# A gated mix of a state-space layer and an MLP on one core: the first two pairs of w1 tiles by halves of 256 tokens

## The chip, the cores and the metric

The kernel runs on one core of a Trainium2 chip. The metric is the device time of one execution in microseconds (us); lower is better. The engines are called by the profile's names: PE (TensorE's matmuls), PEld (its weight loads), DVE (VectorE), ACT (ScalarE), POOL (GpSimd) and SP (SyncE, which here only issues DMAs). SPq, ACTq and POOLq are the queues on which these engines issue DMAs.

## The reference

The input x has 2048 tokens of 448 values in bf16. Three things are computed from it and mixed:

```python
def _A_ref(x, Lambda_re, Lambda_im, B_re, B_im, C_re, C_im, log_dt, Dskip):
    ...
    dt = jnp.exp(log_dt)
    Lam_bar = jnp.exp(dt * Lam)                      # 448 complex poles
    B_bar = ((Lam_bar - 1.0) / Lam)[:, None] * Bmat
    Bu = jnp.einsum("bld,pd->blp", x + 0j, B_bar)    # 448 -> 448 complex
    for t in range(L):
        h = Lam_bar[None, :] * h + Bu[:, t, :]
        hs.append(h)
    y = 2.0 * jnp.einsum("blp,dp->bld", hseq, Cmat).real + x * Dskip[None, None, :]
    return y

def _B_ref(x, w1, w2):
    h = jnp.einsum("bsd,df->bsf", x, w1)             # 448 -> 1792
    h = _silu(h)
    return jnp.einsum("bsf,fd->bsd", h, w2)          # 1792 -> 448

g = _sigmoid((x * gate_w).sum(-1, keepdims=True))
return g * a + (1 - g) * b                           # a = _A_ref, b = _B_ref
```

## The kernel before

**Tiles and stages.** The tokens are cut into four chunks of 512 (`CH`). x lies in `xnat` with tokens on partitions (16 blocks of 128) and is transposed on PE into `xT`, with features on partitions. The 448 features are cut at columns 0, 128, 256 and 320 (`XCOL`) into four pieces `i`; the pieces of `xT` are used by halves of 64 partitions, and two matmuls of 64 rows, one on the upper and one on the lower rows of the array, run beside each other, for two different output tiles. Such a pair of tiles takes 14 matmuls of 64 x 128 weights and 512 tokens, 7 for each tile: first four pairs of matmuls (`part[0]`), then three (`part[1]`), in which the two tiles have changed rows. An output tile is 128 columns of w1 (kind `F`, 14 of them a chunk) or 128 rows of B (kind `B`, 7 of them).

`x_products` (L654) makes these products for a list of tiles, two at a time. `steps(k, h, a, z)` is one group of matmuls of pair `k`; `half(k, h)` is its first or second half, and after the second `evict` takes the two PSUM banks to SBUF: `F` tiles through SiLU on ACT into `aT`, `B` tiles into `UG`. The halves of neighbouring pairs alternate: first half of pair k+1, then second half of pair k. The later stages are `lanes` (the recurrence, as a rotation by COS and SIN, a scan on DVE and a rotation back), `ffn2` (L775, the product with w2), `readout_weights` and `readout` (L796, the product with C), and `gates`.

**The order of the work.** A planner (`Plan`) holds a list of operations with costs, priorities and what they read and write. PE takes its operations in exactly the order in which the code adds them; on SP, ACT, DVE and POOL the planner picks, by its own costs, the operation that can start first and, among these, the one of lowest priority number. `Waits` turns the result into one instruction list per engine with semaphore waits. An engine runs its list in order: an instruction that waits holds all behind it. PE does not wait for itself, except in an operation marked `own`: there it waits until its earlier writes to the bank are done (the second half of a pair adds to a bank from the other rows).

**The start, which the change touches.** Loads (all from `load`, L387 to L390) are issued in the order of their priority numbers: x's tokens 0 to 255 (`xn00`) on SP and 256 to 511 (`xn01`) on ACT; the first 256 columns of w1 (`w1cuts[0:2]`, tiles 0 and 1 of kind `F`) as pieces 0 and 1 on SP, piece 2 and piece 3 on ACT; three rows of parameters (`prm`) on SP; then on SP w1's columns 256 to 511, 512 to 767 and 768 to 1023, two loads each, then B (`Bnat`, which lies in the buffer of `H[3]`; the real part, then the imaginary part `A_B_im`), the rest of w1, the gate and skip vectors, and the rest of x, w2 and C. POOL begins with an iota and a compare that make the identity matrix `ident` (L443, L444), then an iota and cast for the phase (L445, L446), and signs.

PE begins with `warm` (L461): `NWARM` = 6 matmuls of ones with 512 columns and one with 256, whose result is not used. Then come four groups of eight transposes, `x0_transposes(q0, part, who)` (L468 to L478), two for each 256 tokens (`part` 0 and 1), two for the pieces 0, 1 and 2, 3. Each group goes to two banks, and a copy on DVE ("d") or ACT ("a") takes each into `xT` (L486, L488). Then `fill` (L497 to L499), two matmuls of ones with 256 columns, and then the first half of the first pair, cut in two for the loads of w1.

`parameters` (L536) turns the three rows `prm` into columns: a copy of 64 of their columns on DVE (L545), four small matmuls on PE (L543), a copy (L547), and then a long chain on POOL, DVE and ACT that ends in `COS`, `SIN` and the scale factors. It is added behind the first half of the first pair. `b_transposes` (L600 to L611) transposes B in two batches among the products of the third to fifth pair; the second needs the last load of `A_B_im`.

Of the kernel before, what the change touches and what calls it, by code (L numbers as in the profile page):

```python
# [8 lines left out]
AF = mybir.ActivationFunctionType  # L9
# [13 lines left out]
NOT = 5  # L23
NWARM = 6
NFILL = 2
# [251 lines left out]
def bass_gated_mix__ssm_conv_s5__dense_activation_silu__prompt_kernel(nc, A_x, A_Lambda_re, A_Lambda_im, A_B_re, A_B_im, A_C_re, A_C_im,  # L277
               A_log_dt, A_Dskip, B_x, B_w1, B_w2, gate_w, out):
    with ExitStack() as ctx:
# [78 lines left out]
        def bk(t, k=0):  # L358
            return ps[:, t.bank + k, :]
# [22 lines left out]
        def PE(fn, r, w, cost, tag=""):  # L382
            return P.add("pe", fn, r, w, cost, 0, tag=tag)
# [16 lines left out]

        for h, q in enumerate(("sp", "act")):
            load(q, xnat[:, 2 * h:2 * h + 2, :], x2[256 * h:256 * h + 256, :].rearrange("(b p) d -> p b d", p=128), f"xn0{h}", 256 * 896)
        load_w1("sp", 0, 0, 2)
        load_w1("act", 0, 2, 3)
        load_w1("act", 0, 3, 4)
        for k, v in enumerate((A_log_dt, A_Lambda_re, A_Lambda_im)):
            load("sp", prm[k:k + 1, 0:448], v.rearrange("(o n) -> o n", o=1), f"prm{k}", 896)
        for k in range(1, len(w1cuts) - 2):
# [59 lines left out]
        def x0_transposes(q0, part, who):  # L468

            tk = Ps(2)  # L470

            def mm(pe):
                for q in (q0, q0 + 1):
                    for k in range(2):
                        o = ((q - q0) * 2 + k) * 64
                        for h in range(2):
                            p = slice(64 * h, 64 * h + 64)
                            r = pe.transpose(bk(tk, h).bitcast(BF16)[:, o:o + 64], xnat[p, 2 * part + k, XCOL[q]:XCOL[q] + 128], ident[p, p])  # L478
# [12 lines left out]
        x0_transposes(0, 1, "da")  # L491
        x0_transposes(2, 0, "da")
        x0_transposes(2, 1, "dd")

# [7 lines left out]
        xn_of = {tc: {q: [f"xT{tc}_{h}" for h in range(2)] for q in range(4)} for tc in range(1, NCH)}  # L502
        xn_of[0] = {q: [f"xT0_{q}{part}{h}" for part in range(2) for h in range(2)] for q in range(4)}

# [31 lines left out]
        def parameters():  # L536
# [4 lines left out]
            def prm_t(pe):  # L541
                for b in range(4):
                    r = pe.matmul(bk(tkp)[:, 4 * b:4 * b + 3], prm[0:3, 128 * b:128 * b + 128], ident[0:3, 0:3], start=True, stop=True)  # L543
# [110 lines left out]
        def x_products(tiles, fill={}, wait=()):  # L654
# [9 lines left out]

            def steps(k, h, a, z):
                def body(pe):
                    for n, cut in list(enumerate(part[h]))[a:z]:
                        for b, ((i, p0), tile) in enumerate(zip(cut, pairs[k])):
                            tc = tile[1]
                            r = pe.matmul(bk(toks[k], b), weights(tile, p0, p0 + 64, i), xT[p0:p0 + 64, i, tc * CH:(tc + 1) * CH],  # L670
                                          start=(h == 0 and n == 0), stop=(h == 1 and n == 2))
                    return r
                reads = [n for cut in part[h][a:z] for (i, _), tile in zip(cut, pairs[k])
                         for n in xn_of[tile[1]][i] + (w1n(tile[2], i) if tile[0] == "F" else btn[tile[2]])]
                return PE(body, list(dict.fromkeys(reads)), [toks[k]], (z - a) * PE_MM[512], f"{pairs[k][0][0]}{pairs[k][0][1]}")

            def half(k, h):
                if h == 0 and pairs[k][0] == ("F", 0, 0):
                    steps(k, 0, 0, 2)
                    steps(k, 0, 2, 4)  # L680
                else:
                    steps(k, h, 0, len(part[h])).own = h == 1
                if h:
                    evict(pairs[k], toks[k])

            half(0, 0)
            for f in fill.get(-1, ()):
                f()
            for k in range(len(pairs)):
                order = [lambda: half(k, 1)] + [lambda: half(k + 1, 0)] * (k + 1 < len(pairs))  # L690
# [229 lines left out]
```

## Time and profile before

| what | before |
|---|---|
| time, three runs | 142.47, 143.05, 144.9 us; median 143.05 us |
| the profiled execution: its time, and its span | 142.07 us, 140.2 us |
| PE busy | 136.7 us, 97% of the span |
| DVE, ACT, POOL busy | 123.2, 89.0, 38.7 us |
| products with w1 and B (L670), busy | 48.6 + 25.8 us |
| products with w2 (L775), busy | 43.4 us |
| products with C (L796), busy | 16.4 us |
| DMA moved | 14.71 MB, 105 GB/s on average |

The span runs from the first to the last instruction that the profile counts; the execution's own time is 1.87 us longer. Busy time of PE counts each matmul from its start to its modelled end, and two matmuls on different rows overlap, so the mean time of one matmul is longer than the distance from one to the next. The timeline gives start, length, engine, line, operation and operands of merged neighbours; in brackets stands how long the engine had been idle, and what released it. A stage table gives for stretches of time the busy share of each engine, the share of the DMA engines and the GB/s that they moved. Times in the text are from the span's start.

### The profile page before, as it was taken

The page shows a single profiled execution, that of the slowest core. Times are in us where ns is not written, and L with a number is a line of the kernel's source. Part 1 is how long each engine was busy: PE and PEld are TensorE (multiplying, and loading weights), DVE is VectorE, ACT ScalarE, POOL GpSimd, SP SyncE. Part 2 cuts the span into 40 slices and gives each one's busy share as a digit, 9 for nine tenths or more (in the row PEclk, how much of TensorE's full clock was granted, in tenths as well). Part 3 has the DMA queues.
Part 4 walks back from the last instruction along what each step waited for, and adds up shares of the span by engine and source line. Part 5 has one row for each costly group of instructions (what it writes and reads, how often), then busy time and mean ns, then how long its engine had stood idle before and what let it go on. Part 6 is the DMA issues. An engine that isn't in the chain of part 4 may idle for free.

```text
span 140.2 us, 3002 instructions
## 1 busy us (share of the span) xinstructions
PE 136.7 (97%) x1199; PEld 67.5 (48%) x1199; DVE 123.2 (88%) x179; ACT 89.0 (63%) x155; POOL 38.7 (28%) x72
## 2 busy tenths in 40 slices
PE   7999999999999999999999999999999999999992
PEld 2445554445544544455554544444455555555561
DVE  0369999999999999999999999999699999599153
ACT  3239758999998998713971886899920068412300
POOL 7160004201545600229560002833000204222220
PEclk9999999999999999999999999999999999999999
DMA  4988999820447730108975000947001402245342
GB/s 142 262 254 251 320 380 271 201 55 0 69 78 123 126 45 0 37 0 127 158 142 139 0 5 0 134 92 115 2 2 57 106 0 37 33 98 120 46 94 70
DMA packets 18500, 14.71 MB, mean 105 GB/s; under 512 B 2867, under 2 KB 18358, under 8 KB 18486
## 3 DMA queue, kind: packets, MB, share of 16 engines
q0 software_dynamic: 6064, 5.51, 24.7%
q1 hardware_dynamic: 11862, 8.65, 20.4%
q10 hardware_dynamic: 560, 0.36, 0.8%
q8 instruction: 9, 0.15, 0.5%
q14 instruction: 5, 0.04, 0.1%
HBM read 7.17 MB, written 1.84 MB: 64 GB/s over the span
## 4 chain that ended last, share of the span: by engine, by line
PE 97%; DVE 0%; issue 0%
PE ps L670 46%; PE ps L775 31%; PE ps L796 15%; PE ps L463 2%; PE ps L515 1%; PE ps L478 1%; PE ps L815 1%; PE ps L611 1%; PE ps L499 0%; DVE ot L799 0%; PE ps L464 0%; PE ps L543 0%
## 5 line engine op out<-in xcount | busy, mean ns | idle before, releaser
L670 PE MATMUL ps<-xT,w1s 64*128 64x512 bf16 x392 | 48.6, 380 | 0.0
L775 PE MATMUL ps<-w2s,aT 128*128 128x448 bf16 x224 | 43.4, 353 | 0.0
L641 ACT ACTIVATE aT<-ps 128x1024 bf16<-128x1024 f32 (+1 forms) x30 | 28.7, 970 | 10.8 <-PE ps L670 10.6
L775 PEld LDWEIGHTS ps<-w2s,aT 128*128 128x128 bf16 x224 | 21.6, 98 | 20.7 <-issue 0.8
L670 PEld LDWEIGHTS ps<-xT,w1s 64*128 64x128 bf16 x392 | 20.0, 95 | 22.7 <-issue 1.2
L670 PE MATMUL ps<-xT,BT 64*128 64x512 bf16 x196 | 25.8, 376 | 0.0
L783 POOL DMA_DIRECT2D xnat<-fe x16 | 13.9, 889 | 38.1 <-ACT fe L781 35.7
L781 ACT ACTIVATE fe<-ps,g 128x448 bf16<-128x448 f32 x16 | 10.1, 633 | 21.8 <-PE ps L775 17.8
L390 POOL DMA_DIRECT2D UG<-Gf x27 | 15.1, 566 | 30.4 <-DVE Gf L737 30.0
L737 DVE TENSOR_TENSOR_SCAN Gf<-rc,gin,H 128x512 f32<-128x512 f32 x14 | 17.0, 1268 | 0.0
L796 PE MATMUL ps<-CP,H 128*128 128x448 bf16 (+2 forms) x98 | 16.4, 326 | 0.0
L670 PEld LDWEIGHTS ps<-xT,BT 64*128 64x128 bf16 x196 | 11.1, 94 | 10.8
L799 DVE SCALAR_TENSOR_TENSOR ot<-ps,g,xnat 128x448 bf16<-128x448 f32 (+2 forms) x18 | 10.8, 626 | 4.6 <-issue 3.3
L705 DVE TENSOR_TENSOR H<-UG,COS 128x3584 bf16<-128x3584 bf16 (+4 forms) x10 | 12.7, 1272 | 0.0
L796 PEld LDWEIGHTS ps<-CP,H 128*128 128x128 bf16 x98 | 8.9, 98 | 7.5 <-issue 0.4
L649 ACT ACTIVATE UG<-ps 128x1024 bf16<-128x1024 f32 (+1 forms) x12 | 10.7, 916 | 1.8 <-PE ps L670 1.8
L705 DVE TENSOR_TENSOR PO<-UG,SIN 128x1536 bf16<-128x1536 bf16 (+1 forms) x8 | 8.7, 1091 | 2.9 <-ACT UG L747 1.5
L390 POOL DMA_DIRECT2D UG<-UG x8 | 4.6, 580 | 23.0 <-ACT UG L649 11.6
L850 ACT ACTIVATE xnat<-xnat,g 128x448 bf16<-128x448 bf16 x16 | 10.0, 665 | 0.2
L843 ACT ACTIVATE junk<-xg 128x448 bf16<-128x448 bf16 x16 | 9.2, 573 | 0.2
L705 DVE TENSOR_TENSOR PI<-UG,SIN 128x512 bf16<-128x512 bf16 (+2 forms) x13 | 9.2, 730 | 0.0
L737 DVE TENSOR_TENSOR_SCAN Gf<-rc,gin,H2C 128x512 f32<-128x512 f32 x7 | 8.5, 1269 | 0.0
(102 smaller groups left out, 124.9 us busy)
## 6 DMA issues: line engine op xcount, KB each, us to landing
UG<-Gf POOLq DMA_DIRECT2D x21, 128.0 KB, 2.4
xnat<-fe POOLq DMA_DIRECT2D x16, 112.0 KB, 2.8
out_dram<-ot SPq DMA_DIRECT2D x15, 112.0 KB, 1.7
w2s<-in_B_w_dram SPq DMA_DIRECT2D x1, 1568.0 KB, 11.6
xnat<-in_A_x_dram SPq DMA_DIRECT2D x3, 448.0 KB, 7.6
w1s<-in_B_w_dram SPq DMA_DIRECT2D x4, 192.0 KB, 3.4
w1s<-in_B_w_dram SPq DMA_DIRECT2D x1, 576.0 KB, 6.4
UG<-UG POOLq DMA_DIRECT2D x8, 64.0 KB, 2.3
```

The costliest lines, as they stand in the source:

```text
L390: P.add(q, lambda e: e.dma_start(dst, src), list(after), name.split(), 0.6 if q == "pool" else 0.5, prio, sem(), nbytes, tag="ld " + name)
L641: ACT(lambda e, src=src, dst=dst: e.activation(dst, src(), AF.Silu), [tk, "tbl"], [f"aT{tc % 2}_{m}" for m in names], act_cost(512 * n), 2 ...
L649: ACT(lambda e, src=src, dst=dst: e.activation(dst, src(), AF.Copy), [tk], [f"{un}{m}" for m in names], act_cost(512 * n), 5, "U")
L670: r = pe.matmul(bk(toks[k], b), weights(tile, p0, p0 + 64, i), xT[p0:p0 + 64, i, tc * CH:(tc + 1) * CH], start=(h == 0 and n == 0), stop=( ...
L705: DVE(lambda e: e.tensor_tensor(o, a, b, op), r, w, dve_cost(n, 2), prio, tag)
L737: DVE(lambda e, s=s, b=b, init=init: e.tensor_tensor_scan(Gf[:, s, :], rc[:, b:b + 1].to_broadcast([128, CH]), A[:, s, :], init, ALU.mult, ...
L775: r = pe.matmul(bk(tk)[:, 0:D_MOD], aT[tc % 2][:, fb, o:o + 128], w2s[:, fb, :], start=(fb == 0), stop=(fb == NFB - 1))
L781: ACT(lambda e: e.activation(f[:, :], bk(tk)[:, 0:D_MOD], AF.Copy, scale=g1[:, tb:tb + 1]), [tk, f"g1_{tc}"], [fn], act_cost(448, 1), 7, "fe")
L783: P.add("pool", lambda e: e.dma_start(Tb[:, tb, :], f[:, :], accum_op=ALU.add), [fn, f"Tb{tb}"], [f"Tb{tb}"], 0.94, 2, sem(), 115000, tag= ...
L796: r = pe.matmul(bk(tk)[:, 0:b - a], H[tc][:, s, o:o + 128], CP[:, s, a:b], start=(s == 0), stop=(s == NSLOT - 1))
L799: DVE(lambda e, tk=tk, a=a, b=b: e.scalar_tensor_tensor(ot[tb % NOT][:, a:b], bk(tk)[:, 0:b - a], g[:, tb:tb + 1], Tb[:, tb, a:b], ALU.mul ...
L850: ACT(lambda e, tb=tb: e.activation(Tb[:, tb, :], xnat[:, tb, :], AF.Copy, scale=g[:, tb:tb + 1]), [f"xd{tc}", f"g_{tc}"], [f"Tb{tb}"], ac ...
```

## The change

- `NWARM` is 5 instead of 6.
- x's first 256 tokens are two loads of 128 tokens (`xn000` on SP, `xn001` on ACT); tokens 256 to 511 (`xn01`) are one load on SP behind w1's first columns. `gates` names the three loads.
- The three parameter rows are loaded on POOL's queue, with a priority number that puts them behind `ident` and ahead of the other iotas. (POOL's form of the load is cut in 16 pieces of 28 values.)
- The transposes of tokens 256 to 511 come behind the first products. `fill` lies between the first transposes and the first products.
- `steps` takes `of`, the halves of 256 tokens that it works on. In the chunk that begins with tile 0, the first two pairs of tiles are made by halves of 256 tokens in an order written out in `begin`: 28 pairs of matmuls of 256 tokens instead of 14 of 512. Each bank is begun and ended in each half of its columns for itself. The third pair's first half stands ahead of the last piece of the second pair, as before.
- The parameters' matmuls stand behind eleven pairs of matmuls of 256 tokens; before, behind four of 512. Their copy of 64 columns is on ACT instead of DVE.

On SP the three loads of parameters are gone and one of x is added. On PE, ACT, DVE and POOL the order behind these stages is the same, but for a few neighbouring operations that the planner exchanges.

```diff
-NWARM = 6
+NWARM = 5
...
-        for h, q in enumerate(("sp", "act")):
-            load(q, xnat[:, 2 * h:2 * h + 2, :], x2[256 * h:256 * h + 256, :].rearrange("(b p) d -> p b d", p=128), f"xn0{h}", 256 * 896)
+        for b, q in enumerate(("sp", "act")):
+            load(q, xnat[:, b, :], x2[128 * b:128 * b + 128, :], f"xn00{b}", 128 * 896)
         load_w1("sp", 0, 0, 2)
         load_w1("act", 0, 2, 3)
         load_w1("act", 0, 3, 4)
+        load("sp", xnat[:, 2:4, :], x2[256:512, :].rearrange("(b p) d -> p b d", p=128), "xn01", 256 * 896)
         for k, v in enumerate((A_log_dt, A_Lambda_re, A_Lambda_im)):
-            load("sp", prm[k:k + 1, 0:448], v.rearrange("(o n) -> o n", o=1), f"prm{k}", 896)
+            load("pool", prm[k:k + 1, 0:448], v.rearrange("(o n) -> o n", o=1), f"prm{k}", 896, 0.5)
...
-            PE(mm, [f"xn0{part}", "ident"], [tk], 4 * 0.054, "xT0")
+            PE(mm, xn0[part] + ["ident"], [tk], 4 * 0.054, "xT0")
...
+        xn0 = [["xn000", "xn001"], ["xn01"]]
         x0_transposes(0, 0, "da")
-        x0_transposes(0, 1, "da")
         x0_transposes(2, 0, "da")
-        x0_transposes(2, 1, "dd")
...
-            DVE(lambda e: e.tensor_copy(prm[:, 448:512], prm[:, 384:448]), prmn + ["xT0_211"], ["prm4"], 0.17, 0)
-            PE(prm_t, prmn + ["prm4", "ident"], [tkp], 0.5, "prmT")
+            ACT(lambda e: e.activation(prm[:, 448:512], prm[:, 384:448], AF.Copy), prmn + ["xT0_011"], ["prm4"], 0.23, 0)
+            PE(prm_t, prmn + ["prm4", "ident"], [tkp], 0.27, "prmT")
...
-            def steps(k, h, a, z):
+            def steps(k, h, a, z, of=(0, 1)):
+                t0, t1 = 256 * of[0], 256 * of[-1] + 256
                 def body(pe):
                     for n, cut in list(enumerate(part[h]))[a:z]:
                         for b, ((i, p0), tile) in enumerate(zip(cut, pairs[k])):
-                            tc = tile[1]
-                            r = pe.matmul(bk(toks[k], b), weights(tile, p0, p0 + 64, i), xT[p0:p0 + 64, i, tc * CH:(tc + 1) * CH],
-                                          start=(h == 0 and n == 0), stop=(h == 1 and n == 2))
+                            o = tile[1] * CH
+                            r = pe.matmul(bk(toks[k], b)[:, t0:t1], weights(tile, p0, p0 + 64, i), xT[p0:p0 + 64, i, o + t0:o + t1],
+                                          start=(h == of[0] and n == 0),
+                                          stop=(h != of[0] and n == len(part[h]) - 1))
...
+            def begin():
+                steps(0, 0, 0, 2, (0,))
+                steps(0, 0, 2, 4, (0,))
+                x0_transposes(0, 1, "da")
+                x0_transposes(2, 1, "dd")
+                steps(0, 1, 0, 3, (0,)).own = True
+                steps(1, 0, 0, 4, (0,))
+                for f in fill.get(-1, ()):
+                    f()
+                steps(0, 1, 0, 3, (1,))
+                steps(1, 1, 0, 3, (0,)).own = True
+                steps(0, 0, 0, 4, (1,)).own = True
+                evict(pairs[0], toks[0])
+                steps(1, 1, 0, 3, (1,))
+                half(2, 0)
+                steps(1, 0, 0, 4, (1,)).own = True
+                evict(pairs[1], toks[1])
+            k0 = 0
+            if pairs[0][0] == ("F", 0, 0):
+                begin()
+                k0 = 2
+            else:
+                half(0, 0)
+            for k in range(k0, len(pairs)):
...
-            xnn = ["xn00", "xn01"] if tc == 0 else [f"xn{tc}"]
+            xnn = xn0[0] + xn0[1] if tc == 0 else [f"xn{tc}"]
```

More of the change, by code (lines that the diff above doesn't have):

```diff
@@ L502, in bass_gated_mix__ssm_conv_s5__dense_activation_silu__prompt_kernel @@
         xn_of = {tc: {q: [f"xT{tc}_{h}" for h in range(2)] for q in range(4)} for tc in range(1, NCH)}
-        xn_of[0] = {q: [f"xT0_{q}{part}{h}" for part in range(2) for h in range(2)] for q in range(4)}
         def x_transposes(tc, who):
@@ L672, in body @@
                     return r
                 reads = [n for cut in part[h][a:z] for (i, _), tile in zip(cut, pairs[k])
-                         for n in xn_of[tile[1]][i] + (w1n(tile[2], i) if tile[0] == "F" else btn[tile[2]])]
-                return PE(body, list(dict.fromkeys(reads)), [toks[k]], (z - a) * PE_MM[512], f"{pairs[k][0][0]}{pairs[k][0][1]}")
+                         for n in ([f"xT0_{i}{t}{u}" for t in of for u in range(2)] if tile[1] == 0 else xn_of[tile[1]][i])
+                         + (w1n(tile[2], i) if tile[0] == "F" else btn[tile[2]])]
@@ L677, in half @@
+                return PE(body, list(dict.fromkeys(reads)), [toks[k]], (z - a) * PE_MM[512] * len(of) / 2, f"{pairs[k][0][0]}{pairs[k][0][1]}")
             def half(k, h):
[L678 to L682, printed above, removed]
+                steps(k, h, 0, len(part[h])).own = h == 1
                 if h:
                     evict(pairs[k], toks[k])
-            half(0, 0)
@@ L687, in x_products @@
-            for f in fill.get(-1, ()):
-                f()
-            for k in range(len(pairs)):
+            def begin():
[15 more added lines that the diff above has]
+                evict(pairs[1], toks[1])
```

## The prediction

> **What bounds the kernel now.** I read the page's busy shares first, then the chain that ended last, then the timeline of the first 16 us, then the DMA list. The first and fourth parts of the page say that one engine sets the time:
>
> ```profile
> PE 136.7 (97%) x1199; PEld 67.5 (48%) x1199; DVE 123.2 (88%) x179; ACT 89.0 (63%) x155; POOL 38.7 (28%) x72
> ...
> PE 97%; DVE 0%; issue 0%
> ```
>
> The chain lies on PE (TensorE) for 97% of the span; PE never waits for DVE or ACT in it. So an edit counts only if it takes PE time away, or moves PE work to a place where it costs less. The chain in order of time shows where PE does anything but the two big products, and it is at the start:
>
> ```profile
> 0.76 2.72 PE ps L463 x6
> 3.48 0.21 PE ps L464
> ...
> 3.70 1.12 PE ps L478 x29
> 4.82 0.54 PE ps L499 x2
> 5.36 1.59 PE ps L670 x7
> 6.95 0.18 PE ps L543 x4
> 7.13 3.99 PE ps L670 x36
> ```
>
> Columns: start, length, line, instructions. Until 3.69 PE multiplies ones by ones (L463, L464); then it transposes x (L478), fills (L499), and reaches its first useful product at about 5.3. The first 8 useful matmuls run two by two (a pair of 64-row tiles at a time): 4 pairs in about 1.6 us, 0.43 us a pair (their weight loads start at 5.29, 5.70, 6.12). The next 36, 18 pairs, take 3.99 us: 0.22 a pair, and 0.216 over the long stretches (7.57 us for 35 pairs). So PE runs at half speed until some 6.8 us, though the page's PEclk row shows 9 everywhere; two listings of the same line, by shape, for 4 to 7.2 us and for 7.2 to 11 us, show the same:
>
> ```profile
> L670 PE MATMUL ps<-xT,w1s 64*128 64x512 bf16 x10 | 2.0, 527 | 0.0
> ```
> ```profile
> L670 PE MATMUL ps<-xT,w1s 64*128 64x512 bf16 x36 | 4.1, 377 | 0.0
> ```
>
> Everything this change can win lies before 7.13 us: after it PE goes from product to product. What starts PE is the loads:
>
> ```profile
> 0.72 0.48 ACTq L390 DMA_DIRECT2D xnat<-in_A_x_dram  x1
> 0.72 0.43 SPq L390 DMA_DIRECT2D xnat<-in_A_x_dram  x1
> ...
> 1.21 0.46 SPq L390 DMA_DIRECT2D w1s<-in_B_w_dram  x1
> 1.23 0.99 ACTq L390 DMA_DIRECT2D w1s<-in_B_w_dram  x2
> ...
> 2.70 2.93 SPq L390 DMA_DIRECT2D w1s<-in_B_w_dram  x6
> ...
> 3.70 0.96 PEld L478 LDWEIGHTS ps<-ident,xnat 64*128 64x128 bf16 x32 [0.70 <-DMA xnat<-in_A_x_dram]
> ```
>
> The first transpose is released by x's load (2.9 us from issue on SP, 3.2 on ACT, by the DMA list), as the warm-up ends.
>
> **The change, part by part.** *Loads.* x's first 256 tokens become two loads of 112 KB on SP and ACT where two of 224 KB stood. The stage table gives 283 GB/s for 2 to 3 us and 348 for 3 to 4, and 30 for 1 to 2: all of x (459 kB) has moved at 3.4 and landed at 3.9, 0.5 later; half of it has moved at 2.7, so I take 3.2 for its landing (bounds 2.9, SP's 3.6 less 0.7 us of traffic, and 3.7, no gain). w1's first columns have 224 KB less ahead of them, 0.7 us at 320 GB/s: SP's part at 3.9 instead of 4.6 and ACT's two at 4.2 and 4.6 instead of 4.9 and 5.3. x's other half is behind 480 KB; with it 704 KB have moved, which before were there with ACT's last load at 5.3; by rate (313 kB at 3.0, 330 GB/s on) it is 4.2 plus 0.5. I take 5.0, with 4.7 and 5.3 as ends.
>
> *PE until 7.1 us.* One warm-up matmul fewer ends the warm-up at 3.26 instead of 3.69. Then 16 transposes instead of 32 (1.05 us for 32 before, 0.53 for 16): 3.3 to 3.8. Fill, 2 x 0.21: to 4.2. By then the two copies of xT (0.29 on DVE, 0.38 on ACT, started 0.44 after the first transpose as before) and SP's w1 are there. Two half-width pairs at 0.21: to 4.65; the ACT copy of the second group and ACT's last w1 load come at 4.6; two more: to 5.1. Transposes of the other half: 5.1 to 5.6 (5.3 to 5.85 at the late end). Three half-width pairs of the first two tiles: to 6.25. Four of the next two tiles, whose w1 columns landed before at 6.1 (issue 2.70 plus 3.4) and are issued some 0.5 us sooner: at half speed to 6.7, then at full speed, done by 6.95. The parameter transposes, 0.18: 7.13.
>
> So at 7.13 us PE has done 11 half-width pairs, worth 5.5 full ones, where it had done 4. The rest of its list is the same work: 1.5 x 0.216 = **0.32 us less**. Splitting 14 pairs into 28 costs no stream time (half the columns each) and twice the weight loads; PE's loader is 48% busy, and 32 loads of this size are done in 0.47 us in the later transposes (L515), 15 ns each, under a half pair's 0.108 us: nothing, or at worst 0.03 us for the starts. The new waits of PE for itself (a group that adds onto a bank that the group before wrote from the other rows) each have 16 transposes or three half pairs, at least 0.32 us, between writer and waiter; without that cover the wait would be about the 0.24 us that one transpose matmul lasts from start to end, four times at most.
>
> *Parameters.* SP loses three issues of prm (1.72 to 2.70 in the timeline, 0.98 us) and gains one of x (0.43 to 0.5): everything behind comes 0.5 us earlier on SP. POOL issues the three after `ident` (done at 1.72). The trace has no small load from DRAM on POOL; its nearest rows are DMAs within the chip, 566 to 889 ns each on POOL and 2.4 to 2.8 us to landing (5.3 the longest). Issue ends at 3.4 to 4.4; the last is issued at 2.9 to 3.5 and lands at 5.3 to 6.3, I take 5.4, at the worst 8.8. The copy of 64 columns moves from DVE (0.17) to ACT (0.23), behind the copy of xT from the second transposes, at about 6.4. PE wants it at 6.95: covered by 0.3 us or more; a landing at 8.8 would stop PE, with all products behind it, for 2 us. On POOL, the iota and cast for the phase (L445, L446, done at 2.92) and the signs (done at 4.34) wait 1.7 to 2.7 us; DVE reads the first at 9.19. Nothing.
>
> *After 7.13.* The order on PE, ACT, DVE and POOL is the same but for a few neighbours exchanged; the first eviction comes after 10.5 pairs' worth instead of 11 and the second after 18 as before. One place can take the gain back: the second batch of B's transposes (L611) waits for A_B_im.
>
> ```profile
> 6.71 1.22 SPq L390 DMA_DIRECT2D H<-in_A_B_im_dram  x2
> ...
> 11.97 0.55 PEld L611 LDWEIGHTS ps<-ident,H 64*128 64x128 bf16 x32 [0.34 <-issue]
> ```
> ```profile
> H<-in_A_B_im_dram SPq DMA_DIRECT2D x1, 336.0 KB, 4.6
> ```
>
> The second of the two is issued at 7.3, and 4.6 later is 11.9; PE's loader begins at 11.97. PE reached it without slack. In the new order PE gets there at 11.7. The load is issued 0.5 us sooner, and the stage table leaves room (DMA shares of 0.73, 0.91, 0.82 and 0.96 between 5 and 9 us, 0.58 us unused): it can land at 11.4. I count the gain in full; the low bound is 0.03 us (no earlier landing), the high one 0.55 us (full speed from the start of the useful products: they begin 1.1 us sooner, at half speed).
>
> **Sum.** The profiled execution took 142.07 us, span 140.2 and 1.87 around it; less 0.32 gives 141.75. The median of the runs shown is 143.05, 0.98 above the profiled one; the same saving gives 142.73. I predict **142.7 us**, likeliest case alone 142.3 to 143.1.
>
> **Rivals.**
> 1. *Given back at B's transposes.* PE stops at L611 until A_B_im lands at 11.9: 0.03 us left, 143.0. For it: the arrival without slack. Against it: the earlier issue and the free DMA time.
> 2. *Full speed comes later: slower.* Place: PE between 3.3 and 7 us. Before, PE works from 0.76 without a gap worth naming and is at full speed at 6.8, 6.0 us after its first matmul and 2.05 after the last transpose (4.75). Now the ones-product is shorter, the transposes are in two parts, and PE may idle at two places for loads (up to 0.3 us each). If the 2.05 us count from the end of the second transposes (5.6), full speed comes at 7.65, 0.85 later; each us at half speed loses 0.5: 0.43, and the gain is gone with 0.1 on top. If all 6.0 us count anew from there, it comes at 11.6: 2.4 lost less 0.32, 2.1 slower. Between these, 1.1 slower: 144.1. It decides from a delay of 0.65 us on. Against it: before, 32 transposes in one run and a start at 0.76 did not keep PE from full speed.
> 3. *The parameters come late*, at 8.8: PE waits 2 us at the parameter transposes, less the 0.32 gained: 144.7. For it: no such load in the trace. Against it: all neighbours land sooner.
> 4. *The change does not do what it says*: x's first half lands no sooner than 3.7. Then all of PE's start moves by 0.4 at half speed: 0.12 us won, 142.9. I hold this with the first.
>
> [...]
>
> **How the numbers follow.** Forecast 0.57; rivals 1 and 4 together 0.20; rival 2 0.15; rival 3 0.04; something not seen 0.04. The range goes down to 141.4 (gain 0.55 and a median as low as the runs around 142) and up to 144.5 (rivals 2 and 3 at their middle). A change of 2%, 2.9 us, is about what a measurement of this kernel can tell from none; the runs before differ by 2.4. No case won reaches that; of the losses only a missed start of rival 2 at its far end or a very late parameter. Faster 0.03, within 0.90, slower 0.07.
>
> **What would show it.** First transpose at 3.2 to 3.4; first product of 256 columns at about 4.2; second transposes at 5.0 to 5.4; L542's matmuls at 6.9 to 7.2 with 22 half-width matmuls ahead of them; B's second transposes at 11.7 and no PE idle before them. I am wrong if matmuls still last 0.21 us per half pair after 7.2, if PE idles before the parameter transposes, or if the chain shows another engine between 7 and 140 us.

## The result, and the profile after

The changed kernel is slower: 143.75 us median of 22 runs (142.52 to 145.75) against 142.58 for the kernel before in the same rounds (22 runs, 141.77 to 145.16). The ratio is 1.0068, with a 95% interval of 1.0038 to 1.0097. I had forecast 0.32 us less; it is about 1 us more. The ratios and their intervals leave out the runs that were more than 1.5% above the fastest of the same kernel (three of the changed kernel's 22, four of e6's 10 and two of e14's 6 below), while the medians hold all runs. The profiled execution of the changed kernel took 142.7 us, its span 140.9; before it was 142.07 and 140.2.

The busy shares of the page look as before, and PE's busy time is even less (136.0 instead of 136.7 us):

```profile
PE 136.0 (97%) x1226; PEld 68.8 (49%) x1226; DVE 122.9 (87%) x178; ACT 89.3 (63%) x156; POOL 40.2 (29%) x75
```

What is new is that PE waits. The view of PE's waits over the whole span of after (sum in us, times, longest) names one load, which stands in no such row of before:

```profile
PE ps L673 <- DMA w1s<-in_B_w_dram: 1.2, 3, 0.6
```

The timeline of PE's instructions shows where (start, length, engine, line, operation, operands; in brackets the idle time before and its releaser). L673, L610 and L542 are the lines that were L670, L611 and L543:

```profile
3.20 0.61 PE L479 MATMUL ps<-ident,xnat 64*128 64x64 bf16 x16
...
4.62 0.39 PE L673 MATMUL ps<-xT,w1s 64*128 64x256 bf16 x4 [0.31 <-DMA w1s<-in_B_w_dram]
5.58 0.40 PE L673 MATMUL ps<-xT,w1s 64*128 64x256 bf16 x4 [0.56 <-DMA w1s<-in_B_w_dram]
5.79 0.41 PE L479 MATMUL ps<-ident,xnat 64*128 64x64 bf16 x16
...
6.85 0.61 PE L673 MATMUL ps<-xT,w1s 64*128 64x256 bf16 x8 [0.32 <-DMA w1s<-in_B_w_dram]
7.61 0.23 PE L542 MATMUL ps<-ident,prm 3*128 3x3 bf16 x4
7.78 3.76 PE L673 MATMUL ps<-xT,w1s 64*128 64x256 bf16 x50
...
12.37 0.63 PE L610 MATMUL ps<-ident,H 64*128 64x64 bf16 x32
```

The first transposes come early, as forecast, the first products at 4.62 (5.29 before, 4.2 forecast). Then every step waits for a load: w1's first pieces, ACT's last piece, the second columns. PE is at full speed here from 4.1 us on (a half-width group of four lasts 0.4 us), 2.7 us earlier than in the forecast, which was luck, and still starts the long run of products at 7.78, where 7.13 was forecast. The second transposes of B come at 12.37, where 11.7 was forecast and 12.00 was before.

A sign of being wrong that the prediction names shows too: the chain that ended last, on PE for 97% before, now has another engine in it. Between 37 and 50 us it runs over a DMA and ACT, whose copies of the third chunk's `xT` end at 50.24 and let PE go on (start, length, what):

```profile
PE 80%; ACT 9%; DMA 6%; SPq 1%; issue 1%; POOL 0%; DVE 0%; ACTq 0%
```
```profile
48.40 1.84 ACT xT L524 x2
50.29 8.38 PE ps L673 x76
```

### The profile page after: what moved, and what is told of

Its sections match the earlier page's. It is cut to its first block, busy times and chain, and to the rows that moved or that the text cites. A ratio compares the mean times of both kernels' runs of the same rounds, so it can differ in the third digit from the quotient of the medians.

```text
span 140.9 us, 3056 instructions
## 1 busy us (share of the span) xinstructions
PE 136.0 (97%) x1226; PEld 68.8 (49%) x1226; DVE 122.9 (87%) x178; ACT 89.3 (63%) x156; POOL 40.2 (29%) x75
## 3 DMA queue, kind: packets, MB, share of 16 engines
q0 software_dynamic: 6160, 5.51, 24.7%
q1 hardware_dynamic: 12000, 8.76, 20.9%
## 4 chain that ended last, share of the span: by engine, by line
PE 80%; ACT 9%; DMA 6%; SPq 1%; issue 1%; POOL 0%; DVE 0%; ACTq 0%
PE ps L673 39%; PE ps L798 25%; PE ps L819 15%; DMA xnat<-fe 3%; DMA w1s<-in_B_w_dram 3%; ACT aT L640 2%; ACT xT L524 1%; ACT xnat L873 1%; ACT fe L804 1%; SPq L390 1%; ACT junk L866 1%; ACT ct L846 1%; ACT ct L849 1%; PE ps L514 1%; PE ps L610 1%
## 5 line engine op out<-in xcount | busy, mean ns | idle before, releaser
L673 PE MATMUL ps<-xT,w1s 64*128 64x512 bf16 (+1 forms) x420 | 48.7, 362 | 1.3 <-DMA w1s<-in_B_w_dram 1.2
L673 PEld LDWEIGHTS ps<-xT,w1s 64*128 64x128 bf16 x420 | 21.2, 94 | 23.1 <-issue 1.2
L673 PE MATMUL ps<-xT,BT 64*128 64x512 bf16 x196 | 25.8, 376 | 0.0
L804 ACT ACTIVATE fe<-ps,g 128x448 bf16<-128x448 f32 x16 | 10.1, 634 | 23.7 <-PE ps L798 17.2
L673 PEld LDWEIGHTS ps<-xT,BT 64*128 64x128 bf16 x196 | 11.4, 94 | 10.5
L390 POOL DMA_DIRECT2D UG<-UG x8 | 4.3, 547 | 22.0 <-DVE UG L646 11.4
L866 ACT ACTIVATE junk<-xg 128x448 bf16<-128x448 bf16 x16 | 9.3, 578 | 0.5 <-DVE xg L728 0.3
## 6 DMA issues: line engine op xcount, KB each, us to landing
w2s<-in_B_w_dram SPq DMA_DIRECT2D x1, 1568.0 KB, 11.4
```

Source lines behind the costliest of these rows:

```text
L390: P.add(q, lambda e: e.dma_start(dst, src), list(after), name.split(), 0.6 if q == "pool" else 0.5, prio, sem(), nbytes, tag="ld " + name)
L673: r = pe.matmul(bk(toks[k], b)[:, t0:t1], weights(tile, p0, p0 + 64, i), xT[p0:p0 + 64, i, o + t0:o + t1], start=(h == of[0] and n == 0), ...
L804: ACT(lambda e: e.activation(f[:, :], bk(tk)[:, 0:D_MOD], AF.Copy, scale=g1[:, tb:tb + 1]), [tk, f"g1_{tc}"], [fn], act_cost(448, 1), 7, "fe")
L866: ACT(lambda e, tb=tb, b=b: e.activation(junk[:, :], xg[:, b, :], AF.Copy, accum_out=zl[:, tb:tb + 1]), ["xg"], ["junk", f"zl{tc}"], act_c ...
```

## The experiments

I read three things in each trace, since the median hides them. *Ready*: when PE has 5.5 pairs of products behind it and goes on (in kernels with the new order, the start of the row of 50 half-width matmuls; with the old order, the start of the row of 36 plus 1.5 pairs of 0.216 us). *Full from*: when PE goes to full speed, by the trace's own record of PE's clock. *GB/s*: what the DMA engines moved from 3 to 5 us, by a stage table.

| kernel | loads, PE order | full from | ready | GB/s | ratio (95%) |
|---|---|---|---|---|---|
| before | before, before | 6.59 | 7.39 | 332 | 1 |
| after | after, after | 4.14 | 7.78 | 231 | 1.0068 (1.0038–1.0097) |
| e9 | after, after (same kernel) | 12.5 (by durations) | 8.76 | 195 | 1.0099 (1.0068–1.0130) |
| e1 | after, after; later order as before | 10.30 | 8.88 | 215 | 1.0157 (1.0115–1.0199) |
| e2 | after, but parameters on SP; after | 4.98 | 7.66 | 217 | 1.0093 (1.0061–1.0124) |
| e3 | after, before | 4.49 to 7.91, again from 11.32 | 9.09 | 202 | 1.0201 (1.0166–1.0237) |
| e4 | before, after | 3.95 | 7.07 | 311 | 1.0033 (1.0009–1.0056) |
| e5 | before, before; no wait for B | 5.42 | 6.78 | 319 | 0.9930 (0.9905–0.9956) |
| e10 | after, w1 on SP and x's rest on ACT; after | 4.12 | 7.18 | 300 | 1.0086 (1.0061–1.0112) |

(e3's 1.5 pairs are counted at half speed.) Three columns are from one execution each; only the ratio is from many.

### Loads and order apart: e1 to e4, e9, e10

My first theory had two losses: the loads at the start, and a later one. Around 41 us ACT takes one more gate sum (L866) ahead of a scaled product with w2 (L804), its copies of the third chunk's `xT` begin at 48.30 instead of 47.60, and in the waits between 28 and 60 us the row of the weight loads that wait for them is twice as long in after as in before:

```profile
PEld ps L670 <- ACT xT L525: 0.3, 1, 0.3
```
```profile
PEld ps L673 <- ACT xT L524: 0.6, 1, 0.6
```

e1 puts the later order back by changing only a cost that the planner sees, at B's first transposes:

```diff
-PE(mm, [...], [tk], n * 4 * 0.0285, "BT")
+PE(mm, [...], [tk], n * 4 * 0.0285 + (0.30 if s0 == 0 else 0.0), "BT")
```

> The changed kernel with one number of the planner's costs raised by 0.3 (B's first transposes), which alters no instruction and puts ACT's, DVE's and POOL's later operations back into the order that they had before the change. In the two profiled executions PE is 0.40 us behind before when it starts B's second transposes' successors, and 0.64 behind from 50 us on: 0.24 us are lost between, where PE waits for ACT's copy of the third chunk's xT. Theory 'two losses' (start and later order): 0.2 to 0.3 us of the loss come back, ratio to before about 1.006, and PE is as far behind at 58 us as at 13. Rival 'start alone' (the 0.24 us follow from the late start whatever the order): no change against the changed kernel, ratio about 1.008.

Measured: 1.0157, 144.48 us. The row is back at 0.3 in the trace and the chain back on PE (94%), yet the kernel is no faster than after (its interval, 1.0115 to 1.0199, even lies above after's); the later order isn't what makes the change slow. e1's trace shows another loss instead: PE at half speed until 10.3.

e2 is after with the parameters on SP, behind x's other half (and a planner cost of 0.25 as in e1):

```diff
-load("pool", prm[k:k + 1, 0:448], ..., f"prm{k}", 896, 0.5)
+load("sp", prm[k:k + 1, 0:448], ..., f"prm{k}", 896)
```

> The changed kernel with the three parameter rows on SP's queue again, behind x's other half, and the later order as before the change. In the changed kernel's profile the parameters land at 5.9 to 6.9 us on POOL's queue, 4 us after their issue, and the landings of w1's first columns are spread over 1.3 us instead of 0.55. Theory 'POOL's queue' (its small packets hold up the others and come late themselves): w1's first columns land 0.5 us sooner, PE's waits for w1 fall from 1.2 us to under 0.5, and the ratio to before is 0.998 to 1.002. Rival 'the other loads' (three loads of x and their places are to blame): PE still waits about 1 us for w1 in the first 7 us, everything behind on SP's queue is issued 0.5 us later than in the changed kernel, and the ratio is 1.005 to 1.010.

1.0093, 143.62 us. Against after it wins nothing; against e1, on the same chip, it is better by 0.9 us, with intervals that overlap. The loss does not rest on the parameters' queue.

e3 is before with all of after's loads, PE's order untouched; e4 is after with before's loads and `NWARM` 6, the order alone (with the planner cost of e2):

> The kernel before with the change's loads alone: x's first 512 tokens in three loads, the parameters on POOL's queue; PE's order and warm-up as before. Theory 'loads' (the loads are what costs): PE must wait for x's other half at its third group of transposes, until about 5.6 us where it was at 4.0, and first products begin at 6.3 instead of 5.3; ratio 1.004 to 1.008. Rival 'order' (the order of PE's work and its split into halves cost): ratio 0.998 to 1.002.

> The change's order of PE's work alone: the loads, the parameters' queue and six warm-up matmuls as before, and the later order as before. x's two halves land at 3.7 and 4.0, w1 at 4.6 to 5.3, as before. Theory 'loads': PE waits about 0.3 us for w1 once and then has all it needs; ratio 0.996 to 1.000. Rival 'order': ratio 1.004 to 1.010. Rival 'clock' (transposes split in two parts and gaps keep PE at half speed for longer): matmuls of half width still start 0.21 us apart after 7.5 us in the profile, and the times are spread over more than 2 us.

e3: 1.0201, 145.03 us, far above the forecast of either theory. e4: 1.0033, 142.98 us, between its two. This is the clearest pair: the loads without the order that was made for them cost 2%, the order on the old loads 0.3%. In e3 PE stops for x's other half, and the run of 36 products after it lasts 5.46 us instead of 4.06:

```profile
6.30 0.52 PE L479 MATMUL ps<-ident,xnat 64*128 64x64 bf16 x24 [2.27 <-DMA xnat<-in_A_x_dram]
...
8.44 5.46 PE L672 MATMUL ps<-xT,w1s 64*128 64x512 bf16 x36
```

e9 runs the changed kernel once more for a second profile.

> The changed kernel once more, beside the following three. Ratio to before 1.005 to 1.016 (1.0068 at first, 1.0157 with the later order as before). Theory 'first waits': in its profile w1's fourth piece and x's other half, the last loads of ACT's and SP's first batch, land at 5.4 to 6.4 us and PE waits over 0.4 us for them at its second pair of half-width products; where PE idles more than about 1 us between two switching moments of the clock, matmuls after 7 us are still or again at half speed.

1.0099, 144.09 us; the profiled execution took 145.2, 2.5 more than that of after, with the same instructions:

```profile
6.10 0.61 PE L673 MATMUL ps<-xT,w1s 64*128 64x256 bf16 x4 [0.85 <-DMA w1s<-in_B_w_dram]
...
8.76 5.51 PE L673 MATMUL ps<-xT,w1s 64*128 64x256 bf16 x50
```

Against after's rows, ACT's last w1 piece releases PE 0.52 later, the long run begins 0.98 later and lasts 1.75 longer (5.51 against 3.76): together 2.73 us at its end, which covers the whole difference. Of it 0.52 us is a late load; most of the rest is half speed until some 12.5 us. The later loss does not appear here: the order on every engine is after's, and the chain is on PE for 94%.

e10 moves x's other half to ACT, right behind x's first, and w1's four pieces to SP, with e1's planner cost:

```diff
+load("act", xnat[:, 2:4, :], ..., "xn01", 256 * 896)
-load_w1("act", 0, 2, 3)
-load_w1("act", 0, 3, 4)
-load("sp", xnat[:, 2:4, :], ..., "xn01", 256 * 896)
+load_w1("sp", 0, 2, 3)
+load_w1("sp", 0, 3, 4)
```

> The changed kernel (with the later order as before) with other queues for the first loads: all four pieces of w1's first columns on SP behind its part of x, x's other half on ACT behind its part of x. Theory 'first waits' (w1's fourth piece, third in ACT's queue and moved beside x's other half, comes 0.8 us later than I took, and this is the first cost): the piece lands by 5.0 us, x's other half by 4.8, PE's waits in the first 7 us fall below 0.5 us, and the ratio to before is 1.000 to 1.004. Rival: small loads on POOL's queue hold everything up whatever the queues: PE still waits about 1 us, ratio 1.010 to 1.016.

1.0086, 143.54 us. x's other half lands at 4.65 instead of 5.66, the fourth w1 piece at 5.20 instead of 5.44, and PE is ready at 7.18, 0.6 sooner than in after. In this execution PE then stops at B:

```profile
12.47 0.64 PE L610 MATMUL ps<-ident,H 64*128 64x64 bf16 x32 [0.53 <-issue]
```

The profiled execution is the fastest of the six, though: 142.51 us, which is the median of before in those rounds. What holds the median at 143.54 it cannot show.

### The wait for B: e5, e6, e12, e15

B's imaginary part (`A_B_im`) lands last at 11.6 to 13.7 us in these traces, whatever the start does: 11.91 in before, 12.24 in after, 13.09 in e2, 12.38 in e10, and in e4 13.61, where PE had come early:

```profile
13.70 0.64 PE L609 MATMUL ps<-ident,H 64*128 64x64 bf16 x32 [1.88 <-issue]
```

(The releaser "issue" is the landing 0.09 earlier.) To price this, e5 is before with the second transposes reading row blocks of B's real part, which are there, so that they wait for no load; the later row blocks of B are left out of the result.

```diff
-pe.transpose(..., Bnat[p, s0 + q, XCOL[i]:XCOL[i] + 128], ident[p, p])
+pe.transpose(..., Bnat[p, q if q < 3 else 2, XCOL[i]:XCOL[i] + 128], ident[p, p])
...
-PE(mm, [f"H3_{s}" for s in range(s0, s1)] + ["H3_3i"] * (s0 <= 3 < s1) + ["ident"], ...)
+PE(mm, [f"H3_{s}" for s in range(3)] + ["ident"], ...)
```

> The kernel before, with B's second transposes reading the first three row blocks of B's real part in place of the later ones, so that they wait for no further load; part of B is wrong in this kernel, all loads and all work are there. In the profiles so far PE begins these transposes 0.06 to 0.09 us after the last landing of A_B_im: 11.91 and 11.97 before, 12.24 and 12.30 in the changed kernel, 13.09 and 13.18 with the parameters on SP, 13.61 and 13.70 with the change's order alone, where PE had been idle for 1.88 us. Theory 'floor' (the start ends when A_B_im lands, and what PE saves ahead of it is given back): this kernel is faster than before by 0.3 to 1.2 us, ratio 0.992 to 0.998, and PE does not stop at these transposes. Rival 'clock' (only the moment of full speed sets the start): within 0.2 us of before, ratio 0.999 to 1.001.

0.993, 141.51 us (141.24 to 141.81). It wins 1.1 us and most of the spread, with the same instructions in the same order on every engine, so the gain is this wait. In its profiled execution PE did these transposes at 11.35, while the load landed at 13.66:

```profile
6.46 4.06 PE L670 MATMUL ps<-xT,w1s 64*128 64x512 bf16 x36
...
11.35 0.63 PE L611 MATMUL ps<-ident,H 64*128 64x64 bf16 x32
```

So the start of the kernel before ends, in most executions, not with PE's work but with this landing. That is read from the medians: in the one trace of before PE comes to these transposes 0.06 us after the landing and does not stop.

The same edit on e1 (e6), on e4 (e12), and on before with the parameters' matmuls two pairs later (e15, with the planner cost of e2):

> The changed kernel (with the later order as before) with the same edit: B's second transposes wait for no further load; part of B is wrong in it. Theory 'floor': it gains 0.3 to 1 us on the kernel with the later order alone (ratio to before 1.0157 there), where full speed comes early. Theory 'clock': where PE waits for w1 and x at 5 to 6 us the full speed comes after 9 us in many runs, PE reaches the transposes after A_B_im anyway, and the ratio stays at 1.010 or above. Either way, if the change saved time ahead of this place, this kernel would have to be faster than the kernel before without that wait; I expect it slower by 0.5 to 1.5 us.

> The change's order of PE's work alone, with loads as before, and B's second transposes without their wait (part of B is wrong in it). With that wait this order had a ratio of 1.0033; the kernel before without it has 0.993. Theory 'floor': without the floor the split into halves shows what it is worth, 0.2 to 0.4 us on the kernel before without the wait: ratio 0.990 to 0.992. Rival 'order' (half-width products, more weight loads and waits of PE for itself cost by themselves): 0.994 to 0.998.

> The kernel before without B's wait (ratio 0.993; part of B is wrong in it), with the parameters' four small matmuls behind two more pairs of PE's products (0.43 us of PE work; the change puts them behind 1.5 more). Theory 'parameters': DVE's chain for the phases comes 0.4 us later against PE, its copy of B's first transposes is late, and PE waits 0.2 to 0.4 us for it: ratio 0.995 to 0.996. Rival 'no cost', as I had it: 0.992 to 0.994.

e6: 1.0086, 144.39 us. e12: 1.0001, 142.35 us. e15: 0.9921, 141.66 us. With no wait for B, before gains 0.7%, the order alone comes to 0.3% less than with it, and the changed kernel, in e1's form, still loses 0.9% to before (1.3% by the medians): its loss does not rest on B's wait. By the ratios e6 is 2.2 us behind e5, more than the 0.5 to 1.5 expected. e15 was to show whether a later place of the parameters' matmuls costs time; none shows.

e12 holds what stays open. Without B's wait the new order should be even with e5 or ahead; it is 0.84 us behind, outside both forecasts. Its one profile is ready 0.62 later (full speed 0.9 us later than in e5, first transposes 0.16 later) and loses 0.22 more ahead of B's first products, which begin at 12.73 instead of 11.87, the weight loads waiting for DVE:

```profile
12.70 0.57 PEld L672 LDWEIGHTS ps<-xT,BT 64*128 64x128 bf16 x8 [0.20 <-DVE Gf L567]
```

Together that would make up the 0.84; but one execution does not show that this is so in most.

### The clock: e16, e7

e16 is e5 with `NWARM` 1 instead of 6, so that PE idles for 2.26 us ahead of its first transposes, to see whether the clock then rises later; all loads stay:

> The kernel before without B's wait (ratio 0.993; part of B is wrong in it), with one warm-up matmul of 512 columns instead of six: PE is idle from 1.4 to 3.6 us. Theory 'clock': full speed comes later in most runs, at 7 to 10 us, each us later costs up to 0.5 us, and the kernel is 0.7 to 1.7 us slower than with six: ratio 0.998 to 1.005. Rival 'loads bind anyway': 0.992 to 0.995.

1.0017, 143.0 us: 0.87% or about 1.25 us more than e5. Full speed came at 8.79 instead of 5.42, and the same 36 products show it:

```profile
3.82 1.10 PE L478 MATMUL ps<-ident,xnat 64*128 64x64 bf16 x32 [2.26 <-POOL sturn L450]
...
7.41 4.72 PE L670 MATMUL ps<-xT,w1s 64*128 64x512 bf16 x36
```

In these two executions full speed comes 3.4 us later, for which durations twice as long (0.43 us a pair against 0.216 in before) would give 1.7, an estimate, and B's second transposes begin 1.62 later (12.97 against 11.35), 0.20 of it from the later first transposes. The 1.25 us are what the ratios give over all executions.

e7 is e1 with matmuls of ones laid into the gaps (four ahead of the second transposes' wait, two ahead of the second tiles), to keep PE busy while it waits.

```diff
+busy(4)      # behind steps(0, 0, 0, 2, (0,))
...
+busy(2)      # ahead of steps(1, 0, 0, 4, (0,))
```

> The changed kernel (with the later order as before) with six more matmuls of ones, 256 columns each, where PE waits for loads: four behind the first two pairs of half width, two ahead of the second pair of tiles. They take 0.11 us each at full speed, 0.21 at half. Theory 'clock' (idle PE time between 4 and 7 us puts the full speed off to 9 to 11 us): full speed comes before 7.2 us in the profile, the runs above 144 us grow rare, and the median falls by 0.5 to 1.5 us against the kernel with the later order alone, to a ratio of 1.003 to 1.010. Rival 'loads alone' (only the waits cost): the same or slower by up to 0.3 us, ratio 1.015 to 1.018.

1.0136, 144.55 us. Its profile is at full speed from 4.83, but ready only at 8.34, since PE waits 0.81 for ACT's w1 piece, which lands at 6.27. The time is e1's within the intervals: the added matmuls save nothing measurable. Whether they held the clock up in most executions, one profile does not show.

### Other places for the loads: e8, e11, e13, e14

If B's landing is the floor, an earlier B should help. e8 is before with w1's third and fourth column loads merged (one step fewer on SP ahead of B); e11 is before with the larger load of `A_B_im` on ACT's queue, behind ACT's first copies of `xT`; e13 loads all of w1 ahead of B and makes all 14 `F` tiles first; e14 is e13's edit on e1.

```diff
-w1cuts = [0, 256, 512, 768, 1024, 1792]
+w1cuts = [0, 256, 512, 1024, 1792]     # e8
...
-NH = 8
+NH = 14                                # e13, e14, with lanes(0) at fill 10
```

> The kernel before, with w1's columns 512 to 1023 as one pair of loads of 1 KB rows instead of two pairs of 512 B rows: SP issues two loads fewer ahead of B. Theory 'floor': B's loads are issued 1 us sooner, A_B_im lands 0.4 to 1 us sooner, and the kernel is faster than before by 0.2 to 0.8 us, ratio 0.994 to 0.999. Rival 'clock', or a bound by DMA traffic that the row length does not touch: 0.999 to 1.002. If w1's columns 512 to 767 come too late, PE waits at the third pair at 8.6 us and the ratio is above 1.002.

> The kernel before with the large load of A_B_im on ACT's queue, issued behind ACT's last copy of xT at about 5.1 us, where SP issues it at 7.3. Theory 'floor': it lands before 11 us, PE does not stop at B's second transposes, and the kernel gains most of what the kernel without that wait gained (ratio 0.993): 0.993 to 0.997, with the runs within 0.8 us of each other. Rival: the loads of w1 that it now runs beside come too late, and PE waits for these at 8.5 to 10 us: ratio 0.998 to 1.004.

> The kernel before with all 14 w1 tiles of the first chunk ahead of the tiles of B, and the rest of w1 loaded ahead of B: B's transposes still stand behind the third pair in PE's order... but with the pairs counted anew they come behind the sixth and seventh, at 15 to 16 us, when A_B_im has long landed. Theory 'floor': 0.5 to 1 us faster than before, ratio 0.993 to 0.997, runs within 0.8 us. Rivals: the rest of w1 comes too late for its products at 11.5 us (0.2 to 0.5 us of waiting), or the recurrence, begun 4 us later, makes PE wait for DVE later on (any size): ratio 1.000 or above, with PE's waits elsewhere than at B's transposes.

> The changed kernel (later order by the same number of the planner's) with that same order and loads for B. If the change saved time that only A_B_im took back, it is now level with or faster than the previous kernel. Theory 'first waits and clock': it is 0.8 to 1.8 us slower than the previous kernel, as the changed kernel is against before, since PE's waits for w1 and x at 5 to 7 us are untouched.

e8: 0.9986 (0.9964 to 1.0008), 142.35 us; e11: 1.0023; e13: 1.0137; e14: 1.0104. In e8, e11 and e13 the wait moves to what now lands last. e8's B lands 0.7 sooner, at 11.22, and PE waits for the merged columns instead:

```profile
8.89 2.55 PE L670 MATMUL ps<-xT,w1s 64*128 64x512 bf16 x22 [0.81 <-DMA w1s<-in_B_w_dram]
```

e11 waits 0.45 for B's real part, and e13 for the rest of w1, with a later wait of 0.5 for DVE on top, which would fit the later recurrence:

```profile
12.03 2.77 PE L670 MATMUL ps<-xT,w1s 64*128 64x512 bf16 x24 [1.36 <-DMA w1s<-in_B_w_dram]
```

e14 was forecast 0.8 to 1.8 us behind e13, and their medians are level, 144.85 and 144.81. By its own words that would speak for the change; but e13's start ends with the rest of w1, while PE in e14, at full speed only from 9.14, does not wait for these columns at all. The new floor hides the start, and the pair decides nothing.

No kernel that computes the whole result is shown to beat before; e8 comes nearest, and its interval holds 1.

## Why the prediction was wrong, by its steps

**Right.** x's first half landed at 2.92 and 3.09 (3.2 forecast) and the first transposes began at 3.2; in e9, the same kernel, these are 3.24, 3.46 and 3.55. In the long run at full speed splitting pairs costs PE nothing to be seen: 17 half pairs at 0.108 and 8 whole ones at 0.216 are 3.56 us, and the row of 50 has 3.76 to its last matmul's end (before, 18 pairs: 3.89 and 4.06). The 0.03 us "for the starts" was my estimate; no run shows it. The parameters' POOL loads landed at 5.89 to 6.94, not at 5.4, yet far from the 8.8 of rival 3; PE's timeline has 0.15 us of idle time ahead of their matmuls.

**The step that failed first: when the loads land ("0.7 us at 320 GB/s", "330 GB/s on", "4.2 plus 0.5").** I let the DMA engines run at before's rate with 224 KB less ahead of w1, and let a load land 0.5 us after all bytes issued up to it have moved. Neither held. From 3 to 5 us the nine traces with before's first loads have 293 to 333 GB/s, the eight with after's (e2 with its parameters on SP among them) 195 to 265. The stage tables for 3 to 4 us, before and then after (length, busy share and count of PE, PEld, DVE, ACT, POOL, then PEclk, DMA share, GB/s), show it at its worst:

```profile
3.00:4.00 1.00, 0.99 (x11) 0.24 (x9) 0.00 (x0) 0.53 (x1) 0.81 (x7) 1.00 1.12 348
```
```profile
3.00:4.00 1.00, 1.00 (x20) 0.59 (x18) 0.36 (x2) 0.79 (x3) 0.99 (x3) 1.00 0.74 164
```

By the tables' GB/s from 1 us on, the 704 KB (721 kB) up to x's other half had moved at 4.65 in after, not at 4.2. That load landed at 5.66, 1.0 later, and by 5.0 already 826 kB had moved: bytes of later loads went ahead of its last ones. Before's own trace has such a gap, 1.07 (721 kB moved at 4.19, ACT's last piece landed at 5.26), where the forecast took 0.5.

So the landings came late: the fourth w1 piece at 5.44 to 6.08 in after, e1, e2 and e9 (4.6 forecast, 4.95 to 5.26 with before's loads), x's other half at 5.66 to 6.32 (5.0), w1's second columns at 6.25 and 6.72 instead of half a microsecond before 6.1. PE waits three times, 1.2 us together, for w1 ahead of the long run, where the sum had no wait.

Why the rate fell stays open. By 2.2 us both kernels had issued the same 704 KB of x and w1, so loads were not lacking; what differs is their order and their queues: before, all 448 KB of x are issued at 0.72; in after half of it is issued at 1.63 on SP, and takes 4.0 us to land. e2, with the parameters back on SP, has the low rate too (217), so these are not its cause; e10, where x's other half is issued on ACT by 1.6 and w1's pieces on SP, has 300. I did not try the two halves of e10 apart. What this step costs in the median is not settled either: after's loads cost 2% under the old order (e3), but e10, which has them nearly in time, is no faster than after.

**The step that failed next: half speed taken as given.** The whole gain was useful work moved into time where PE had been filling at half speed, with full speed at 6.8 in the forecast, read from the durations of one execution. With before's loads and six warm-up matmuls the moment is not fixed: 6.59, 3.95, 5.42, 4.40, 5.86, 6.33, 3.69 and 4.62 in eight traces (before, e4, e5, e8, e11, e12, e13, e15). Where it comes early, the old order is ready at 6.8 (e5) or 6.3 (e13), not 7.39, and products moved ahead meet what is not there yet. With full speed from 3.69 and 3.95 the old order (e13) and the new one (e4) begin their first products at 4.81 and 4.79, and the new one, with waits of 0.28 for ACT's copy of `xT` and 0.15 for w1, is ready at 7.07, not ahead. Moreover rival 2 is real, though not by its trigger: with after's loads, five of eight traces lost full speed or came to it late (e1 10.30, e14 9.14, e9 12.5, e3 back to half at 7.91, e6 at 7.57).

The switch moments in e3 are 4.49, 7.91 and 11.32: 3.42 and 3.41 apart; in e6 they are 4.16, 7.57 and 10.99. What goes with the loss in these traces is not the transposes, since before reached full speed with all 32 of them in the 3.4 us ahead of it (3.70 to 4.82, full from 6.59), but long idle time of PE at loads. The longest wait is 1.02 us in e1, 0.82 in e14, 0.85 in e9, 2.27 in e3 and 1.71 in e6, against 0.56 in after and 0.52 in e2; e7, with 0.81 and matmuls of ones in its gaps, was at full speed from 4.83 and kept it. In e3 PE ran no matmul in 1.8 of the 3.4 us that ended in the fall (from 4.49 to 6.30). How much idle time it takes is open: after waited three times, 1.2 us together, in the 3.41 us from 4.14 to 7.55 and kept full speed, so the "about 1 us" of e9's expectation, an estimate of mine, is not shown. What sets the moments is not shown either. The eight moments with before's loads and six warm-up matmuls span 2.9 us, from 3.69 to 6.59: this kernel's start can't be priced from one profile.

**"I count the gain in full".** Rival 1 was right about the place and too kind: A_B_im did not land at 11.4, but at 11.6 to 13.1 in the kernels with after's PE order and loads, and e5 shows that this landing already ended the start of before. An earlier PE had nothing to win there; e4 and e10 stop at it in their traces, while after's own PE came too late to stop.

**After 7.13 us.** That nothing would change there missed 0.24 us near 48 us in the profile of after (the ACT rows above); e1, without it, does not bring the time back.

**The sum as measured.** In the two profiled executions, PE begins the chain's first stretch of 70 products at 13.00 instead of 12.64, 0.36 later; with 0.04 by 29 us and 0.24 near 48 us the span is 0.64 longer. That execution of after was one with early full speed. (The forecast's 142.7 also started from three runs of before, whose median, 143.05, is 0.47 above that of the 22.) The rest of the 1.17 us between the medians fits executions such as e9's, but how often each occurs, the runs do not tell: late loads and half speed are seen in the traces, their shares of the median are not.

## What to carry to other kernels

When a start is bound by loads, read the last landing that each stage waits for in several executions before moving PE work: here work moved ahead of its loads became a wait (1.2 us for w1 in after), and a gain ahead of a later landing was given back there (e4 stopped 1.88 us for B). Splitting a first load so that its half landed sooner (3.09 us in after, where the whole had landed at 3.9) also changed when the loads behind it landed, here for the worse (w1's fourth piece at 5.44 to 6.08, with before's loads at 4.95 to 5.26); check the landings and the rate in the next two microseconds, not only the landing of the first half. A gain that rests on PE being at half speed needs more than one profile, since that moment wandered here from 3.69 to 6.59 us.

## What the hardware showed that I had not expected

- The same load lands up to 1.75 us apart from one execution to another: with before's loads, `A_B_im` at 11.91 (before), 13.61 (e4) and 13.66 (e5).
- The profile's PEclk row shows full speed from the first slice on (9 in every slice of before), while matmuls last twice as long (0.43 us a pair against 0.216 in before) until 3.7 to 12.5 us; here only durations and the record of switches tell. A later fall does show (0.50 in e3 from 8 to 10 us).
- Loads of 0.9 KB on POOL's queue took 0.48 to 0.71 us each to issue and 4.0 to 4.2 us to land in after. With the last on SP, e2 had them at 5.29 instead of 6.94.
